# Attention reads and an expert layer on one core: the order of quadrant sums, state products and read transposes

## The chip, the cores and the metric

The kernel runs on one core of a Trainium2 chip. The metric is the device time of one execution in microseconds (us), taken as the median of several runs; less is better. The engines are TensorE (PE), VectorE (DVE), ScalarE (ACT), GpSimd (POOL) and SyncE (SP), which only issues DMAs here. Each engine works through its own list of instructions in order, and semaphores order the engines among each other.

## The reference

A cross-attention between a sequence and a small state, in both directions, is followed by an expert layer with an exact gelu. There are 8 batches, 8 heads, 512 positions, 32 state rows and 64 values a head.

```python
scores = scale * x @ state.T            # per batch and head
xread = softmax(scores) @ state         # 512 rows
sread = softmax(scores.T) @ x           # 32 rows
y = concat([xread, sread])              # (8 * 544, 512), heads side by side
g = gelu(y @ w_in)                      # w_in  512 x 2048
out = g @ w_out                         # w_out 2048 x 512
```

## The kernel before

The instruction order is written out by hand: the scheduler leaves the lists as the Python code emits them. Batches 0 and 1 are worked through by a start-up section. A loop then goes over batches b = 2 to 7; one pass is called a slot here, and each slot has eight steps p = 0 to 7 (units 1 to 8).

**State products (P).** Instead of forming the read and then multiplying it by w_in, the kernel multiplies the state by w_in. `p_mm(b, f, tiles)` makes chunk f (512 of the 2048 columns) of batch b: 8 matmuls of 64x32 weights into two PSUM tiles, one for each t (half of the heads). `p_copy` casts tile t = 0 on ACT and t = 1 on DVE to the bf16 tensor P. In most slots all four chunks of the next batch are made in step 5 by `p_all`, together with the state's reads (sr). For batch 2 chunks 0 and 1 are made ahead of the loop, and chunks 2 and 3 in slot 2 by `pmat`.

**Hidden layer.** `M(k, k + 1)` computes two of the 16 blocks (128 hidden values by 512 positions): two matmuls hp from P and the transposed attention weights AT, then a gelu on ACT into g. Block m needs chunk m // 4 of P. Step p makes blocks 2p and 2p + 1.

**Second layer.** g @ w_out runs by seven products of quadrants instead of eight. `X(b, name)` is one product: 16 matmuls xp into one PSUM bank. The names are 3, 4, 5, 2, 1, 6 and 7. Products 5, 2, 1, 6 and 7 need a sum of two quadrants of g, made on DVE by `g_sum` (128 x 2048 bf16, a pool of three buffers), called g5, g2, g1, g6 and g7 below. Product 6 needs only blocks 0 to 7. In slot b steps 0 to 3 and 5 run products 4, 5, 1, 2 and 7 of batch b - 1, step 5 ends with product 3 of batch b and step 7 with product 6 of batch b.

What follows a product: X3 is copied to s3 on ACT; X4 is added on DVE (s34); X5 is copied on ACT (oh), and POOL makes u; X1 is added on DVE (q); X2 is copied on ACT (oh), POOL makes v, and DVE adds (L618); X7 is added on DVE (L654). SP writes the results out.

**State reads.** `reads_mm` computes sr on PE, ACT copies it (sraw), `reads_norm` scales it on DVE to srm; `srt` transposes srm on PE (srT) and DVE copies it into XSR. In the last slot (read-out, batch 7) the rows of all reads go through the expert layer (sp, srx, srw, rp). Slot 6 handles the reads of batches 6 and 7.

**Order of the rest of a slot.** Scores of batch b + 1 come in step 1, the norms in steps 2 and 3 on DVE, the DMA transposes on SP in steps 3 and 5. POOL waits at `hold_for` for a gelu, issues the loads of x and rearranges x (L225 and L235) between its u and v.

**PSUM.** The pool `ps_f` has four buffers, taken in turn by hp, scores, sr, srT and those P tiles that name no place. The pool `ps_o` has four named places o0 to o3, one bank each; X3 and X5 use o0, X4 and X2 use o1, X1 and X7 use o2, X6 uses o3. `p_all` puts chunks 0 to 3 at (o0, ps_f), (ps_f, ps_f), (o1, o3) and (o2, ps_f).

The parts of the slot that matter here, in step order:

```python
M(k, k + 1)
if b == 2 and p in (0, 3):
    pmat(2, 2 + p // 3)
...
    if p == 3:
        g_sum(b, "6")
    X(b - 1, "45127"[p])
```

Of the kernel before, what the change touches and what calls it, by code (L numbers as in the profile page):

```python
# [10 lines left out]
BF16 = mybir.dt.bfloat16  # L11
# [6 lines left out]
def kernel(  # L18
# [8 lines left out]
    nc = tc.nc  # L27

    B, H, S, D = x.shape
    _, _, NS, _ = state.shape  # L30
# [3 lines left out]
    HC = H // 2  # L34
# [13 lines left out]
    ps_f = ctx.enter_context(tc.tile_pool(name="ps_f", bufs=4, space=PSUM))  # L48
# [6 lines left out]
    def otile(shape, name, at=None):  # L55
        if at is None:
            at = turn[0] % 4
            turn[0] += 1
        return ps_o.tile(shape, FP32, name=name, tag=f"o{at}")

    def ftile(shape, name):
        return ps_f.tile(shape, FP32, name=name, tag="f")
# [5 lines left out]
    ident = persist.tile([128, 128], BF16, name="ident")  # L68
    sbd = persist.tile([128, B, HC, 2 * NS], BF16, name="sbd")
    XSR = persist.tile([128, HC, NS, B], BF16, name="XSR")  # L70
# [133 lines left out]
    atts = {}  # L204
# [25 lines left out]
    def rearr_ones(b):  # L230
        A = atts[b]
        eng = nc.vector if b < 2 else nc.gpsimd
        src = xbs[b].rearrange("p (t c) (j d) -> p t c j d", t=2, d=D)
        for t in range(2):
            eng.tensor_copy(  # L235
                out=A.xo[:, :, :, 2 + 64 * t:66 + 64 * t].rearrange("p j c d -> p c j d"),
                in_=src[:, t],
            )
# [174 lines left out]
    def srt(b):  # L413
        A = atts[b]
        ps = ps_f.tile([128, HC, NS], BF16, name="srT", tag="f")
        nc.tensor.transpose(  # L416
            ps.rearrange("p c n -> p (c n)"), A.srm.rearrange("q t d -> q (t d)"), ident
        )
        nc.vector.tensor_copy(out=XSR[:, :, :, b], in_=ps)  # L419

    Ps = {}

    def p_mm(b, f, tiles):
        if b not in Ps:
            Ps[b] = att.tile([128, 2, d_ff], BF16, name="P", tag="P")
        ps = [tiles([128, 512], "p_ps") for t in range(2)]
        for c in range(HC):
            for t in range(2):
                nc.tensor.matmul(  # L429
                    ps[t][32 * c:32 * c + 32, :],  # L430
                    lhsT=sbd[64 * t:64 * t + 64, b, c, 32 * t:32 * t + 32],
                    rhs=w_in_bf[64 * t:64 * t + 64, c, f * 512:(f + 1) * 512],
                    start=True,
                    stop=True,
                )
        return ps

    def p_copy(b, f, ps):
        dst = Ps[b][:, :, f * 512:(f + 1) * 512]
        nc.scalar.copy(out=dst[:, 0, :], in_=ps[0])  # L440
        nc.vector.tensor_copy(out=dst[:, 1, :], in_=ps[1])  # L441

    def pmat(b, f):
        p_copy(b, f, p_mm(b, f, ftile))
# [134 lines left out]
    def g_q(b, h, k):  # L579
        return gs[b][:, MH * k:MH * k + MH, 256 * h:256 * h + 256]  # L580

    def g_sum(b, name):
        (h0, k0), (h1, k1), op = G_SUMS[name]
        t = apool.tile([128, MH, 256], BF16, name="gsum", tag="gsum")
        nc.vector.tensor_tensor(out=t, in0=g_q(b, h0, k0), in1=g_q(b, h1, k1), op=op)  # L585
        xs[b, "g" + name] = t
# [34 lines left out]
    def X(b, name):  # L621
        bank = {"3": 0, "4": 1, "5": 0, "2": 1, "1": 2, "6": 3, "7": 2}[name]
        first = name in "3416"
        if first:
            xs[b, bank] = otile([128, 2, NH], "xp", bank)
        ps = xs[b, bank]
        lhs = {"3": (0, 0), "4": (1, 1)}.get(name)
        lhs = xs[b, "g" + name] if lhs is None else g_q(b, *lhs)
        rhs = {"5": w_q[1][1], "2": w_q[0][0]}.get(name)
        rhs = w_sum[name] if rhs is None else rhs  # L630
        x_mm(ps, lhs, rhs, first)
        if name == "3":
            xs[b, "s3"] = c_tile("s3")
            if b > 1:
                nc.scalar.copy(out=xs[b, "s3"], in_=ps)
            for h in range(2):
                xs[b, "o", h] = hpool.tile([128, 2, d_model], FP32, name="oh", tag=f"oh{h}")
        elif name == "4":
            xs[b, "s34"] = c_tile("s34")
            nc.vector.tensor_tensor(out=xs[b, "s34"], in0=ps, in1=xs[b, "s3"], op=ALU.add)  # L640
        elif name == "5":
            o = xs[b, "o", 0][:, :, NH:]
            nc.scalar.copy(out=o, in_=ps)  # L643
            xs[b, "u"] = c_tile("u")
            x_out(b, 0, right)
            nc.gpsimd.tensor_tensor(out=xs[b, "u"], in0=xs[b, "s34"], in1=o, op=ALU.subtract)  # L646
        elif name == "2":
            nc.scalar.copy(out=xs[b, "o", 1][:, :, :NH], in_=ps)  # L648
            c22(b)
        elif name == "1":  # L650
            xs[b, "q"] = c_tile("q")
            nc.vector.tensor_tensor(out=xs[b, "q"], in0=ps, in1=xs[b, "s34"], op=ALU.add)  # L652
        elif name == "7":
            nc.vector.tensor_tensor(  # L654
                out=xs[b, "o", 0][:, :, :NH], in0=ps, in1=xs[b, "u"], op=ALU.add
            )
            x_out(b, 0, left)
# [268 lines left out]
                op=ALU.mult,  # L926
            )

    def p_all(b, bs):
        raw = reads_mm(bs)  # L930
        done = []
        for f, at in enumerate(((0, None), (None, None), (1, 3), (2, None))):
            it = iter(at)

            def tiles(shape, name):
                i = next(it)
                return ftile(shape, name) if i is None else otile(shape, name, i)

            done.append((b, f, p_mm(b, f, tiles)))
        for x in done:  # L940
            p_copy(*x)
        reads_norm(bs, raw)

    def p_copy_v(b, f, ps):
# [7 lines left out]
    def M(*ms):  # L952
        for m in ms:
            mm1(m // MC, m % MC)
# [198 lines left out]
    for b in range(2, B):  # L1153
        nb = b + 1
        for p in range(8):
            k = 16 * b + 2 * p
            if p == 1 and nb < B:
                scores(nb, 0)
                scores(nb, 1)
            if p in (2, 3) and nb < B:  # L1160
                norm(nb, p - 2)
            if p == 3 and nb + 1 < B:
                xtr_dma(nb + 1)
            if p == 5 and nb < B:
                atr_dma(nb)
            if p == 7 and nb < B:
                srt(b)
                if nb == B - 1:
                    srt(nb)
            if nb == B and p < 5:  # L1170
                read_out_slot(p)
                if p == 4:
                    r_homes()
                    r_sum("5")
                    r_sum("2")
                continue
            M(k, k + 1)
            if b == 2 and p in (0, 3):
                pmat(2, 2 + p // 3)
            if b == 2 and p == 1:  # L1180
                w_sums(4)
            if p < 4 or (p == 4 and nb == B):
                if p == 0:
                    g_sum(b - 1, "5")
                    if b > 2:
                        sr_w("5216"[b - 3])
                if p == 3:
                    g_sum(b, "6")
                X(b - 1, "45127"[p])
                if p < 3:  # L1190
                    g_sum(b - 1, "127"[p])
            if p == 0 and b + 3 < B:
                hold_for(b, 0)
                load_x(4 if b == 2 else b + 3)
            if p == 6 and b == 2:
                hold_for(b, 12)
                load_x(5)
            if p == 0 and nb + 1 < B:
                begin(nb + 1)
                rearr(nb + 1)  # L1200
            if nb == B:
                if p == 5:
                    g_sum(b, "6")
                    R("3")
                    r_sum("1")
                    R("4")
                    r_sum("6")
                    r_sum("7")
                if p == 6:
                    R("5")  # L1210
                    X(b, "3")
                    R("2")
                    R("1")
                if p == 7:
                    R("6")
                    X(b, "6")
                continue
            if p == 5:
                X(b - 1, "7")
                reads = (b, nb) if nb == B - 1 else (b,)  # L1220
                p_all(nb, reads)
                if b == 2:
                    rearr_ones(3)
                elif nb + 1 < B:
                    rearr_ones(nb + 1)
                X(b, "3")
            if p == 7:
                if b == 2:
                    rearr_ones(4)
                X(b, "6")  # L1230
    b = B - 1
    for name in "521":
# [39 lines left out]
```

## Time and profile before

| | us |
|---|---|
| median of 3 runs | 205.29 (205.24 to 205.36) |
| the profiled execution | 205.13 |
| its span in the trace | 203.2 |
| PE busy | 196.0 (96%) |
| DVE busy | 162.9 (80%) |
| ACT busy | 136.6 (67%) |
| POOL busy | 68.4 (34%) |
| DVE quadrant sums (gsum), 35 | 50.2, mean 1.449 |
| DVE casts of P, 29 | 18.3, mean 0.681 |
| ACT casts of P, 29 | 15.3, mean 0.597 |
| DVE copies into XSR, 8 | 5.7, mean 0.758 |

Times in the trace count from the start of the span. The slots begin at about 50 us (slot 2), 73, 95, 116, 137 and 159 us (slots 3 to 7). Rows of a timeline give start, length, engine, line, operation, tiles and shapes and the count of merged instructions; a bracket at the end names idle time before the row and what released it. Matmuls of one kind are pipelined, so their rows overlap by a tail, and start-to-start distances are the pace.

### The profile page before, as it was taken

To read this page: it belongs to the slowest core of one execution; us is meant where nothing else is said; L and a number is where in the kernel's file an instruction comes from. 1 tells how busy PE (TensorE), PEld (TensorE's weight loads), DVE (VectorE), ACT (ScalarE), POOL (GpSimd) and SP (SyncE) were. 2 spreads that over 40 slices of the span, in tenths; PEclk is the share of its full clock that TensorE was granted. 3 is DMA by queue.
4 is the path that set the end of the run, shared out by engine and by line. 5 is a ranking of instruction groups with operands and counts; after the bars stand their busy time and mean duration, and the time that the engine had idled before them with its cause. 6 is when DMAs were issued, how large, how long until landed. Compare 5 with 4: busy or idle time off the path is not lost.

```text
span 203.2 us, 4901 instructions
## 1 busy us (share of the span) xinstructions
PE 196.0 (96%) x2030; PEld 133.9 (66%) x2035; DVE 162.9 (80%) x255; ACT 136.6 (67%) x245; POOL 68.4 (34%) x75
## 2 busy tenths in 40 slices
PE   7899999999999999999999999999999999999993
PEld 2434544466766687666776677677776887878893
DVE  2954876789999889996899777967799888895882
ACT  3785678798985779656967597687857576864120
POOL 8972503324259297430527302420220002200000
PEclk9999999999999999999999999999999999999999
DMA  6999999986655879633772508270107001040134
GB/s 192 199 172 203 206 198 197 185 163 126 89 104 106 206 87 143 135 126 84 94 167 77 133 0 127 39 205 0 52 3 206 3 0 55 0 158 0 52 107 155
DMA packets 40566, 23.16 MB, mean 114 GB/s; under 512 B 21856, under 2 KB 39136, under 8 KB 40544
## 3 DMA queue, kind: packets, MB, share of 16 engines
q0 software_dynamic: 13984, 8.10, 29.3%
q1 hardware_dynamic: 25872, 14.36, 27.7%
q10 hardware_dynamic: 688, 0.39, 0.6%
q8 instruction: 16, 0.26, 0.5%
q14 instruction: 6, 0.05, 0.1%
HBM read 17.30 MB, written 8.91 MB: 129 GB/s over the span
## 4 chain that ended last, share of the span: by engine, by line
PE 68%; DVE 15%; DMA 5%; POOL 4%; issue 4%; ACT 2%; DVEq 0%; POOLq 0%; ACTq 0%
PE xp L591 30%; PE hp L494 20%; DVE gsum L585 6%; DMA xb<-in_x_dram 5%; PE op L536 3%; PE sp L798 3%; PE rp L864 3%; POOL w_in_bf L105 2%; DVE P L441 2%; DVE a L356 2%; PE op L520 2%; PE xp L703 2%; PE p_ps L429 2%; DVE cs L353 1%; PE pt L333 1%
## 5 line engine op out<-in xcount | busy, mean ns | idle before, releaser
L501 ACT ACTIVATE g<-hp 128x512 bf16<-128x512 f32 x124 | 66.3, 606 | 21.5 <-PE hp L494 17.0
L494 PE MATMUL hp<-AT,P 128*128 128x512 bf16 x248 | 62.0, 379 | 0.6 <-DVE P L441 0.4
L591 PEld LDWEIGHTS <-gsum 128*128 128x128 bf16 x528 | 51.4, 98 | 11.4 <-DVE q L652 0.2
L585 DVE TENSOR_TENSOR gsum<-g 128x2048 bf16<-128x2048 bf16 x35 | 50.2, 1449 | 4.1 <-ACT g L501 4.0
L494 PEld LDWEIGHTS <-P 128*128 128x128 bf16 x248 | 23.2, 98 | 21.1 <-issue 2.2
L591 PE MATMUL xp<-ws,gsum 128*128 128x256 bf16 x304 | 36.3, 273 | 0.0
L591 PE MATMUL xp<-ws,g 128*128 128x256 bf16 x224 | 26.8, 273 | 0.2
L591 PE MATMUL xp<-w_out_bf,gsum 128*128 128x256 bf16 x224 | 26.6, 273 | 0.0
L591 PEld LDWEIGHTS <-g 128*128 128x128 bf16 x224 | 21.5, 98 | 5.0 <-issue 1.6
L646 POOL TENSOR_TENSOR u<-s,oh 128x512 f32<-128x512 f32 x6 | 8.8, 1467 | 40.6 <-ACT oh L643 40.6
L225 POOL COPY x<-xb 128x1024 bf16<-128x1024 bf16 x12 | 14.3, 1225 | 16.6 <-DMA xb<-in_x_dram 16.6
L441 DVE CAST P<-p_ps 128x512 bf16<-128x512 f32 x29 | 18.3, 681 | 1.2 <-PE p_ps L429 1.0
L440 ACT CAST P<-p_ps 128x512 bf16<-128x512 f32 x29 | 15.3, 597 | 4.8 <-PE p_ps L429 4.7
L235 POOL COPY xo<-xb 128x1024 bf16<-128x1024 bf16 x12 | 13.2, 1129 | 5.0 <-PE sr L905 5.0
L610 POOL TENSOR_TENSOR v<-q,oh 128x512 f32<-128x512 f32 x6 | 8.2, 1371 | 19.6 <-ACT oh L648 17.2
L356 DVE TENSOR_TENSOR a<-e,ics 128x512 bf16<-128x512 bf16 x14 | 11.7, 833 | 0.5
L536 PE MATMUL op<-w_out_bf,g 128*128 128x512 bf16 x44 | 11.1, 380 | 0.5 <-issue 0.3
L353 DVE TENSOR_REDUCE cs<-e 128x16 f32<-128x512 bf16 x14 | 9.5, 677 | 0.7 <-ACT e L340 0.7
L429 PE MATMUL p_ps<-w_in_bf,sbd 64*32 64x512 bf16 x248 | 9.6, 381 | 0.3 <-DVE oh L654 0.3
L501 ACT ACT_TABLE_LOAD x7 | 9.0, 1283 | 0.1
L419 DVE COPY XSR<-srT 128x128 bf16<-128x128 bf16 x8 | 5.7, 758 | 3.8 <-PE srT L416 3.8
L536 PEld LDWEIGHTS <-g 128*128 128x128 bf16 x48 | 4.1, 97 | 5.9 <-issue 1.1
(137 smaller groups left out, 233.2 us busy)
## 6 DMA issues: line engine op xcount, KB each, us to landing
out_dram<-oh SPq DMA_DIRECT2D x15, 256.0 KB, 2.7
xb<-in_x_dram POOLq DMA_DIRECT2D x7, 512.0 KB, 7.5
out_dram<-oh SPq DMA_DIRECT2D x6, 512.0 KB, 2.8
w_in_bf<-in_moe_w_in_dram POOLq DMA_DIRECT2D x6, 256.0 KB, 11.8
out_dram<-osb SPq DMA_DIRECT2D x5, 256.0 KB, 3.2
w_out_bf<-in_moe_w_out_dram POOLq DMA_DIRECT2D x4, 256.0 KB, 8.0
w_out_bf<-in_moe_w_out_dram POOLq DMA_DIRECT2D x2, 512.0 KB, 13.3
x0f<-in_x_dram SPq DMA_DIRECT2D x3, 256.0 KB, 3.8
```

Source lines behind the costliest of these rows:

```text
L225: nc.gpsimd.tensor_copy(out=A.x4[:, :, :, 64 * t:64 * t + 64].rearrange("p j c d -> p c j d"), in_=src[:, t],)
L235: eng.tensor_copy(out=A.xo[:, :, :, 2 + 64 * t:66 + 64 * t].rearrange("p j c d -> p c j d"), in_=src[:, t],)
L353: nc.vector.reduce_sum(out=cs, in_=e4, axis=AX.X)
L356: nc.vector.tensor_tensor(out=A.a[:, :, hs].rearrange("p g (c n) -> p g c n", n=NS), in0=e4, in1=ics[:, :, :].to_broadcast((128, G, 2, NS) ...
L429: nc.tensor.matmul(ps[t][32 * c:32 * c + 32, :], lhsT=sbd[64 * t:64 * t + 64, b, c, 32 * t:32 * t + 32], rhs=w_in_bf[64 * t:64 * t + 64, c ...
L440: nc.scalar.copy(out=dst[:, 0, :], in_=ps[0])
L441: nc.vector.tensor_copy(out=dst[:, 1, :], in_=ps[1])
L494: nc.tensor.matmul(hp, lhsT=Ps[b][:, t, m * 128:(m + 1) * 128], rhs=atts[b].AT[:, :, t, :], start=(t == 0), stop=(t == 1),)
L501: nc.scalar.activation(out=gs[b][:, m, :], in_=hp, func=AF.Gelu)
L536: nc.tensor.matmul(ops[b, j], lhsT=gs[b][:, m, j * 128:(j + 1) * 128], rhs=w_out_bf[:, m, :], start=(m == 0), stop=(m == MC - 1),)
L585: nc.vector.tensor_tensor(out=t, in0=g_q(b, h0, k0), in1=g_q(b, h1, k1), op=op)
L591: nc.tensor.matmul(ps[:, j - js[0], :], lhsT=lhs[:, m, 128 * j:128 * j + 128], rhs=rhs[:, m, :], start=(first and j == js[0] and m == 0), ...
```

## The change

Four things are different.

1. In `p_all`, tile t = 1 of chunk 0 is cast on ACT instead of DVE. ACT makes five of the eight casts, DVE three.
2. `g_sum(b, "6")` is no longer emitted in step 3 of slots 2 to 6, ahead of X2, but in step 5, behind `p_all` and its norm.
3. `srts` replaces `srt`: the transposes of srm come in step 7 behind that step's two blocks and ahead of X6, no longer ahead of the blocks. In slot 6 both transposes go into one PSUM tile, and one DVE copy takes them.
4. In slot 2, chunks 2 and 3 of batch 2's P are no longer made in steps 0 and 3. Step 2 makes blocks 4 to 7 at once, then X1 and g7, then both chunks in one run of 16 matmuls with their four casts. Step 3 then has no blocks left to make.

The number of matmuls is the same. Five P casts move from DVE to ACT, and one XSR copy fewer remains on DVE.

```diff
+    def srts(bs):
+        ps = ps_f.tile([128, len(bs), HC, NS], BF16, name="srT", tag="f")
+        for i, b in enumerate(bs):
+            nc.tensor.transpose(
+                ps[:, i].rearrange("p c n -> p (c n)"),
+                atts[b].srm.rearrange("q t d -> q (t d)"),
+                ident,
+            )
+        nc.vector.tensor_copy(
+            out=XSR[:, :, :, bs[0]:bs[-1] + 1], in_=ps.rearrange("p b c n -> p c n b")
+        )
...
-    def p_all(b, bs):
+    def p_all(nb, bs):
...
-            done.append((b, f, p_mm(b, f, tiles)))
-        for x in done:
-            p_copy(*x)
+            done.append((nb, f, p_mm(nb, f, tiles)))
+        for b, f, ps in done:
+            for t in range(2):
+                copy = nc.scalar.copy if t == 0 or f == 0 else nc.vector.tensor_copy
+                copy(out=Ps[b][:, t, f * 512:(f + 1) * 512], in_=ps[t])
         reads_norm(bs, raw)
...
-            if p == 7 and nb < B:
-                srt(b)
-                if nb == B - 1:
-                    srt(nb)
...
-            M(k, k + 1)
-            if b == 2 and p in (0, 3):
-                pmat(2, 2 + p // 3)
+            if b != 2 or p != 3:
+                M(k, k + 1)
+            if b == 2 and p == 2:
+                M(k + 2, k + 3)
+                X(1, "1")
+                g_sum(1, "7")
+                for x in [(2, f, p_mm(2, f, ftile)) for f in (2, 3)]:
+                    p_copy(*x)
...
-                if p == 3:
-                    g_sum(b, "6")
-                X(b - 1, "45127"[p])
-                if p < 3:
-                    g_sum(b - 1, "127"[p])
+                if b > 2 or p != 2:
+                    X(b - 1, "45127"[p])
+                    if p < 3:
+                        g_sum(b - 1, "127"[p])
...
                 p_all(nb, reads)
+                g_sum(b, "6")
...
             if p == 7:
                 if b == 2:
                     rearr_ones(4)
+                srts(reads)
                 X(b, "6")
```

## The prediction

> **What bounds the kernel now.** I read the shares first, then the chain of waits, then the timelines of TensorE (PE), VectorE (DVE), ScalarE (ACT) and GpSimd (POOL) around the edited lines.
>
> ```profile
> PE 196.0 (96%) x2030; PEld 133.9 (66%) x2035; DVE 162.9 (80%) x255; ACT 136.6 (67%) x245; POOL 68.4 (34%) x75
> PEclk9999999999999999999999999999999999999999
> ```
>
> PE is the bound, at a full granted clock. No matmul count changes, so the change can only win or lose time in which PE stands. The rows below show where PE stands; all lie before 158 us. The chain of waits from 156.99 us to 195.70 us is PE alone, so what is won before is carried to the end.
>
> Slot 2 (the pass over batch 2), PE timeline; columns are start, length, line, tiles, count, and idle before with its releaser:
>
> ```profile
> 51.16 0.41 PE L429 MATMUL p_ps<-w_in_bf,sbd 64*32 64x512 bf16 x8
> 59.91 0.41 PE L429 MATMUL p_ps<-w_in_bf,sbd 64*32 64x512 bf16 x8
> 62.00 1.46 PE L494 MATMUL hp<-AT,P 128*128 128x512 bf16 x6
> 63.87 0.59 PE L494 MATMUL hp<-AT,P 128*128 128x512 bf16 x2 [0.40 <-DVE P L441]
> 64.30 1.91 PE L591 MATMUL xp<-ws,gsum 128*128 128x256 bf16 x16
> ```
>
> The lengths hold a pipeline tail, so I reckon from start to start: hp costs 0.216 a matmul (x8 is 1.73 in the chain), X 1.75 for x16. Six hp from 62.00 should end at 63.30; the next comes at 63.87, so PE stands 0.57 for DVE's cast of chunk 3.
>
> Slot 3, PE and then DVE:
>
> ```profile
> 88.99 0.41 PE L429 MATMUL p_ps<-w_in_bf,sbd 64*32 64x512 bf16 x8 [0.19 <-DVE oh L654]
> 89.33 1.92 PE L591 MATMUL xp<-ws,g 128*128 128x256 bf16 x16
> ```
>
> ```profile
> 86.52 1.21 DVE L585 TENSOR_TENSOR gsum<-g 128x2048 bf16<-128x2048 bf16 x1
> 87.66 0.68 DVE L618 TENSOR_TENSOR oh<-xp,v 128x512 f32<-128x512 f32 x1
> 88.26 0.68 DVE L654 TENSOR_TENSOR oh<-xp,u 128x512 f32<-128x512 f32 x1
> ```
>
> The first of these is g6 in its old place. It pushes L654, which frees PSUM tag o2, and the last of the four P chunks in `p_all` waits for o2.
>
> Slot 4 (DVE, POOL) and slot 6 (PE):
>
> ```profile
> 112.92 0.74 DVE L922 TENSOR_TENSOR srm<-sraw,inv 128x128 bf16<-128x128 f32 x1
> ```
>
> ```profile
> 111.49 2.03 POOL L225 COPY x<-xb 128x1024 bf16<-128x1024 bf16 x2
> ```
>
> ```profile
> 156.46 0.36 PE L416 MATMUL srT<-ident,srm 128*128 128x128 bf16 x2
> 156.99 1.10 PE L494 MATMUL hp<-AT,P 128*128 128x512 bf16 x4 [0.17 <-ACT g L501]
> ```
>
> In slot 6 two srT tiles make the next hp wait for a buffer that a gelu frees.
>
> **Slot 2, the two P runs joined behind unit 2.** Removed: two runs of x8. The first costs 51.07 (end of the hp from 50.21) to 51.50 (next X), 0.43; the second the same; 0.86 together. Added: one x16 run. The one at 45.88 runs from the hp end at 45.79 to the hp at 46.44: 0.65. Saved 0.21.
>
> Walk PE from 51.07 without gaps: X4 1.75, scores 0.47, two blocks 0.86, X5 1.75, blocks 4 to 7 1.73, X1 1.75, P run 0.65, X2 1.75. That is 61.78; block 8's first half ends at 62.00 and its second needs chunk 2's cast on DVE. DVE's order there is norm, q, g7, then the two casts. X1 ends near 59.4 as against 58.95, and q stood at 59.48 behind norm's multiply anyway, so I leave g7 at 60.09 plus its 1.45, which ends at 61.5. The cast of 0.68 ends near 62.15, and PE goes on at 62.2: a stall of 0.2 replaces the 0.57. X7 starts at 62.2 + 7 x 0.216 = 63.7 or 63.75, against 64.30: **0.55 won**. Lower end: if g7 slides by the 0.45 of X1's shift, 0.1. Upper end: no stall at all, 0.21 + 0.57 = 0.78. I take 0.55, since norm's row bounds q on both sides of the change.
>
> Covers: blocks 6 and 7 take the PSUM buffers of blocks 2 and 3, whose gelus end 56.3 and 56.9 by ACT's rows (the exp table load moves from 52.48 to 52.0 when the cast at 51.87 leaves); PE wants them at 56.8 and 57.2. The P run takes those of blocks 4 to 7, free by 59.3; wanted at 59.5 and 59.7. If one gelu (0.5) is late, 0.1 to 0.3 is lost. Norm's second half and the POOL-fed add L618 queue behind the casts on DVE. L618 then ends near 65.6, L654 near 66.3, the chunk that needs o2 comes at 66.57. SP's transpose of batch 3's weights (median 3.9 to land) is issued about 1.4 later, behind that norm, and would land near 69 for a first use after 72: hidden. POOL's holds, loads and copies keep their order.
>
> **`p_all` in slots 2 to 6, one cast from DVE to ACT.** ACT gains five casts at 0.49 start to start (four take 2.05), DVE loses five at 0.60 (four take 2.47). ACT's cover is its wait ahead of the s3 copy: 1.01 in slot 3, 0.82 in slot 4, 0.58 each in slots 2 and 6, so nothing; uncovered it would be at most 0.49 in a slot, but only through a gelu that PE waits for. The first ACT cast, which frees X3's bank, keeps its place.
>
> **g6 behind `p_all`.** In its old place it goes away from before L618 and L654. Slot 3: L654 then follows X7's end (87.35) and is done near 88.2; the fourth chunk comes at 88.39 (its pace after the third), and X3 is bound by ACT's first cast, 88.27 + 0.59 + 0.06 = 88.92, against 89.33: **0.41 won**. Slot 4 has the same stall: X3 at 110.60 against 110.82, 0.22, but see the next lines. Slots 2, 5 and 6 show no such stall.
>
> In its new place X6 waits for it. From L654's end or the second chunk's latency (0.5 after its matmuls start, as in slot 6): three casts, inv, srm, then g6 1.21. Against X6's natural start:
> - slot 2: g6 done 70.1, X6 at 70.7 (0.5 in hand);
> - slot 3: 92.0 against 92.5;
> - slot 5: 135.4 against 135.9;
> - slot 6, two norms: 157.3 against 157.5;
> - slot 4: casts end 112.1, but srm meets POOL's pair of copies 111.49 to 113.52. Before, srm ended at 113.66 instead of some 0.3 after its start. If it ends there again, g6 ends at 114.8 and X6 starts at 114.86 against 114.81 before: 0.05 lost, and the 0.22 with it. If srm slips in between the copies, the second copy moves by 0.3 and g6 ends at 115.0: 0.24 lost. If neither meets POOL, X6 starts at 114.2: 0.6 won. I take **0.1 lost**, by the srm row.
>
> The Trainium skill (SBUF — State Buffer, Who interferes with whom) speaks against this place: a VectorE instruction with two SBUF inputs and a GpSimd instruction that reads SBUF exclude each other for a whole instruction, and who issues first goes first. The rows of slot 4 agree (srm 0.74 there, 0.29 in slot 3), and so does a gsum of 3.17 beside the POOL copies at 72.29. By the rule alone, whose copies come as a queue of whole instructions, slot 4 loses 0.24 instead of 0.1.
>
> **srT behind the slot's last two blocks.** Slot 6: the hp at 156.99 no longer waits for gelu 12, because srT is allocated after it. Lost there before: 156.99 less 156.72 and the tails, by pace 0.34 + 0.08 = **0.42 won**; 0.49 if the 0.07 between the two transposes also goes, 0 if srT only moves the wait. Its new tile needs gelu 12, done 156.9, wanted 157.3. Slot 4's wait of srT for srm is counted above. The other srT move at no cost (0.06 each). On DVE the XSR copies move behind g6; slot 6 has one of 256 strided elements for two of 0.73 (1.30 together). Between 0.73 and 1.46, I take 1.3: done 159.1, the two srx 159.6, wanted by the first read-out matmul near 160.1. That margin of 0.5 is thin but uncovered only by a late g6.
>
> **Sum.** 0.55 + 0.41 - 0.10 + 0.42 = 1.28. The profiled execution took 205.13 (span 203.2); 205.13 - 1.28 = 203.85. The median 205.29 lies 0.16 above, giving 204.0.
>
> **Rivals.**
> - Slot 4 free (no meeting with POOL): 0.7 more, 203.3. Against it, srm's row.
> - Only half comes: slot 2 wins 0.1 and slot 6 nothing; 0.1 + 0.41 - 0.1 = 0.4, so 204.9. For it: g7 and norm on DVE are already at the limit in slot 2.
> - Nothing arrives: DVE or ACT in the read-out slot 7 eats it, 205.3. PE's gapless chain speaks for slack, but shows only that there is some.
> - Slower: g6 becomes X6's gate in all five slots. Beside a POOL instruction a gsum takes 2.29 (slot 4's old g6), 1.1 more. Margins 0.5, 0.5, 0.5 and 0.2 would turn into losses of 0.6, 0.6, 0.6 and 0.9, and slot 4 into 1.2 in place of 0.1: 3.8 against wins of 1.28 + 0.1, net 2.5, so 207.8. It decides from about 0.75 a slot. Against it: POOL idles at those times in slots 2, 3, 5 and 6 (3.56 before the hold at 70.87, nothing from 89.86 to 96.14, none near 134 or 156).
>
> **How the numbers follow.** Forecast 0.52, slot 4 free 0.16, half 0.15, nothing 0.08, slower 0.09. The range 203.2 to 204.95 takes the first three with their bounds. A difference of 0.2% (0.41) is about what a measurement of this kernel can tell from none: faster 0.80, same 0.10, slower 0.10.
>
> **What would show it.** Right: no wait of hp for P over 0.3 in slot 2, the four P chunks of slots 3 and 4 in one x32 row, hp x8 ahead of srT in slot 6 without a gelu wait, X6 in slot 4 the only one to wait for gsum. Wrong: L591 waiting for DVE gsum L585 at X6 in slots 2, 3, 5 or 6; ACT's s3 copy starting after X3's end by over 0.6; a gap in slot 7, where there was none.

## The result and the profile after

The changed kernel takes 203.93 us (203.59 to 204.46) where the kernel before takes 205.26 (204.95 to 206.0): a ratio of 0.9933, with a 95% interval of 0.9911 to 0.9954. A further comparison of the same two kernels, on one chip, gave 0.9941 (0.9917 to 0.9965). The profiled execution took 203.66, with a span of 201.6.

The shares, from the page of the changed kernel:

```profile
PE 195.0 (97%) x2030; PEld 134.3 (67%) x2035; DVE 156.0 (77%) x249; ACT 138.8 (69%) x250; POOL 68.0 (34%) x75
```

DVE has lost 6.9 us of work, ACT gained 2.2, and the kernel got 1.3 shorter. The shares do not say where; PE's standing time does. Line numbers are those of the changed kernel here: p_ps is L441, hp L506, X is L603, gsum L597, the casts of `p_all` L955.

Slot 2 on PE (start, length, line, tiles, count, idle before):

```profile
59.28 0.62 PE L441 MATMUL p_ps<-w_in_bf,sbd 64*32 64x512 bf16 x16
59.84 1.92 PE L603 MATMUL xp<-w_out_bf,gsum 128*128 128x256 bf16 x16
61.60 0.38 PE L506 MATMUL hp<-AT,P 128*128 128x512 bf16 x1
62.23 1.68 PE L506 MATMUL hp<-AT,P 128*128 128x512 bf16 x7 [0.25 <-DVE P L453]
63.75 1.91 PE L603 MATMUL xp<-ws,gsum 128*128 128x256 bf16 x16
```

The two P runs are one. A wait for a cast is still there: the first half of block 8 starts at 61.60, the second at 62.23 instead of 61.82, so 0.41 is lost where 0.57 was. What the cast waited for is on DVE:

```profile
59.39 0.69 DVE L664 TENSOR_TENSOR q<-xp,s 128x512 f32<-128x512 f32 x1 [0.78 <-PE xp L603]
60.00 1.57 DVE L597 TENSOR_TENSOR gsum<-g 128x2048 bf16<-128x2048 bf16 x1
61.49 1.27 DVE L453 CAST P<-p_ps 128x512 bf16<-128x512 f32 x2
```

DVE stands 0.78 for the end of X1; then q, g7 and only then the casts. In the kernel before, the norm's multiply (`a`) ended later and q followed it without a wait:

```profile
58.54 1.02 DVE L356 TENSOR_TENSOR a<-e,ics 128x512 bf16<-128x512 bf16 x1
59.48 0.68 DVE L652 TENSOR_TENSOR q<-xp,s 128x512 f32<-128x512 f32 x1
60.09 1.45 DVE L585 TENSOR_TENSOR gsum<-g 128x2048 bf16<-128x2048 bf16 x1
```

Slot 3, PE and ACT. The four chunks run as one row of 32. The first of ACT's five casts, which frees X3's bank, ends at 88.28 (87.69 + 0.59), and X3 follows 0.05 later:

```profile
87.22 1.06 PE L441 MATMUL p_ps<-w_in_bf,sbd 64*32 64x512 bf16 x32
88.33 1.91 PE L603 MATMUL xp<-ws,g 128*128 128x256 bf16 x16
```

```profile
87.69 2.54 ACT L955 CAST P<-p_ps 128x512 bf16<-128x512 f32 x5
```

Slot 4, DVE, POOL and PE. This is the one place where X6 waits for g6:

```profile
111.14 0.47 DVE L934 TENSOR_TENSOR srm<-sraw,inv 128x128 bf16<-128x128 f32 x1
111.54 2.05 DVE L597 TENSOR_TENSOR gsum<-g 128x2048 bf16<-128x2048 bf16 x1
```

```profile
110.44 2.08 POOL L225 COPY x<-xb 128x1024 bf16<-128x1024 bf16 x2
```

```profile
113.65 1.92 PE L603 MATMUL xp<-ws,gsum 128*128 128x256 bf16 x16 [0.42 <-DVE gsum L597]
```

The pair of copies ends at 112.52. g6 ends at 113.59, 1.07 after that, so it did next to nothing while the second copy ran (a gsum without a copy beside it takes 1.22). X6 of slot 4 in the kernel before, to which the account of the prediction comes back:

```profile
114.64 1.91 PE L591 MATMUL xp<-ws,gsum 128*128 128x256 bf16 x16
```

Slot 6, PE and DVE:

```profile
154.57 1.89 PE L506 MATMUL hp<-AT,P 128*128 128x512 bf16 x8
156.30 0.28 PE L424 MATMUL srT<-ident,srm 128*128 128x128 bf16 x2
156.41 1.91 PE L603 MATMUL xp<-ws,gsum 128*128 128x256 bf16 x16
```

```profile
156.61 0.43 DVE L429 COPY XSR<-srT 128x256 bf16<-128x256 bf16 x1 [0.35 <-PE srT L424]
```

The four blocks of steps 6 and 7 run without a gap, srT waits for nothing, and one copy of 0.43 stands for two that took 1.30 in the kernel before:

```profile
156.71 1.30 DVE L419 COPY XSR<-srT 128x128 bf16<-128x128 bf16 x2 [0.18 <-PE srT L416]
```

A yardstick without the noise of the kernel's ends is the stretch from the state transposes ahead of slot 2 (the last row of L160) to the start of X6 in slot 6: 109.76 before, 108.41 after, 1.35 less. The table gives it for all kernels, with the two distances in a slot that move: sr (its first matmul) to X3, and X3 to X6. All are start to start in the traces of one execution each, in us.

| kernel | stretch | to sr of slot 2 | slot 2 | slot 3 | slot 4 | slot 5 | slot 6 |
|---|---|---|---|---|---|---|---|
| before | 109.76 | 17.95 | 1.52 + 3.56 | 1.89 + 3.58 | 1.70 + 3.83 | 1.47 + 3.56 | 1.74 + 4.08 |
| changed | 108.41 | 17.59 | 1.52 + 3.53 | 1.47 + 3.53 | 1.47 + 4.11 | 1.47 + 3.53 | 1.74 + 3.58 |
| changed, again | 108.41 | 17.58 | 1.52 + 3.53 | 1.47 + 3.53 | 1.47 + 4.11 | 1.47 + 3.53 | 1.74 + 3.58 |
| slot 2 alone | 110.31 | 17.59 | 2.45 + 3.58 | 1.88 + 3.58 | 1.70 + 3.83 | 1.47 + 3.56 | 1.73 + 4.08 |
| g6 and casts alone | 109.82 | 17.92 | 1.52 + 3.56 | 1.47 + 3.56 | 1.47 + 4.12 | 1.47 + 3.56 | 1.73 + 4.55 |
| srT alone | 108.78 | 17.89 | 1.52 + 3.53 | 1.88 + 3.54 | 1.69 + 3.54 | 1.47 + 3.53 | 1.73 + 3.58 |
| four casts each | 108.85 | 17.59 | 1.52 + 3.53 | 1.47 + 3.53 | 1.47 + 4.26 | 1.47 + 3.53 | 1.74 + 3.87 |
| g6 back | 109.43 | 17.58 | 2.46 + 3.54 | 1.88 + 3.54 | 1.69 + 3.54 | 1.47 + 3.53 | 1.73 + 3.58 |
| batch 7 later | 107.81 | 17.58 | 1.52 + 3.53 | 1.47 + 3.53 | 1.47 + 3.53 | 1.47 + 3.53 | 1.74 + 3.58 |
| casts before g7 | 107.98 | 17.16 | 1.52 + 3.53 | 1.47 + 3.53 | 1.47 + 4.11 | 1.47 + 3.53 | 1.73 + 3.58 |
| both | 107.39 | 17.16 | 1.52 + 3.52 | 1.47 + 3.53 | 1.47 + 3.53 | 1.47 + 3.53 | 1.74 + 3.58 |
| both, again | 107.39 | 17.16 | 1.52 + 3.53 | 1.47 + 3.53 | 1.47 + 3.53 | 1.47 + 3.53 | 1.74 + 3.58 |
| both, srT ahead | 108.50 | 17.16 | 1.52 + 3.56 | 1.47 + 3.56 | 1.47 + 3.56 | 1.47 + 3.56 | 1.74 + 4.55 |

### The profile page after: what moved, and what is told of

The parts are those of the page before. It is cut to its first block, busy times and chain, and to the rows that moved or that the text cites. A ratio compares the mean times of both kernels' runs of the same rounds, so it can differ in the third digit from the quotient of the medians.

```text
span 201.6 us, 4900 instructions
## 1 busy us (share of the span) xinstructions
PE 195.0 (97%) x2030; PEld 134.3 (67%) x2035; DVE 156.0 (77%) x249; ACT 138.8 (69%) x250; POOL 68.0 (34%) x75
## 4 chain that ended last, share of the span: by engine, by line
PE 88%; DVE 6%; ACT 2%; DMA 2%; issue 1%; ACTq 0%
PE xp L603 39%; PE hp L506 26%; PE op L548 5%; PE sp L810 3%; PE rp L876 3%; PE p_ps L441 2%; PE op L532 2%; PE xp L715 2%; DVE gsum L597 2%; DMA st_f<-in_state_dram 2%; PE pt L333 2%; PE sr L917 1%; ACT P L955 1%; DVE P L955 1%; PE hp L1060 1%
## 5 line engine op out<-in xcount | busy, mean ns | idle before, releaser
L506 PE MATMUL hp<-AT,P 128*128 128x512 bf16 x248 | 61.2, 379 | 0.3 <-DVE P L453 0.2
L603 PEld LDWEIGHTS <-gsum 128*128 128x128 bf16 x528 | 51.2, 98 | 11.5 <-DVE gsum L597 0.8
L597 DVE TENSOR_TENSOR gsum<-g 128x2048 bf16<-128x2048 bf16 x35 | 47.5, 1371 | 0.5
L506 PEld LDWEIGHTS <-P 128*128 128x128 bf16 x248 | 23.3, 98 | 21.6 <-DVE P L453 1.0
L603 PE MATMUL xp<-ws,gsum 128*128 128x256 bf16 x304 | 36.3, 273 | 0.4 <-DVE gsum L597 0.4
L603 PE MATMUL xp<-ws,g 128*128 128x256 bf16 x224 | 26.7, 272 | 0.3
L603 PE MATMUL xp<-w_out_bf,gsum 128*128 128x256 bf16 x224 | 26.6, 273 | 0.0
L603 PEld LDWEIGHTS <-g 128*128 128x128 bf16 x224 | 21.8, 98 | 5.3 <-issue 1.6
L235 POOL COPY xo<-xb 128x1024 bf16<-128x1024 bf16 x12 | 12.6, 1080 | 5.0 <-PE sr L917 5.0
L955 ACT CAST P<-p_ps 128x512 bf16<-128x512 f32 x25 | 12.7, 606 | 0.1
L955 DVE CAST P<-p_ps 128x512 bf16<-128x512 f32 x15 | 9.4, 685 | 1.7 <-PE p_ps L441 1.7
L441 PE MATMUL p_ps<-w_in_bf,sbd 64*32 64x512 bf16 x248 | 8.8, 380 | 0.0
L452 ACT CAST P<-p_ps 128x512 bf16<-128x512 f32 x9 | 4.9, 589 | 5.4 <-PE p_ps L441 5.4
L963 POOL COPY hold<-g 128x1 bf16<-128x1 bf16 x5 | 2.9, 575 | 16.9 <-ACT g L513 16.8
```

Source lines behind the costliest of these rows:

```text
L235: eng.tensor_copy(out=A.xo[:, :, :, 2 + 64 * t:66 + 64 * t].rearrange("p j c d -> p c j d"), in_=src[:, t],)
L441: nc.tensor.matmul(ps[t][32 * c:32 * c + 32, :], lhsT=sbd[64 * t:64 * t + 64, b, c, 32 * t:32 * t + 32], rhs=w_in_bf[64 * t:64 * t + 64, c ...
L506: nc.tensor.matmul(hp, lhsT=Ps[b][:, t, m * 128:(m + 1) * 128], rhs=atts[b].AT[:, :, t, :], start=(t == 0), stop=(t == 1),)
L603: nc.tensor.matmul(ps[:, j - js[0], :], lhsT=lhs[:, m, 128 * j:128 * j + 128], rhs=rhs[:, m, :], start=(first and j == js[0] and m == 0), ...
L955: copy(out=Ps[b][:, t, f * 512:(f + 1) * 512], in_=ps[t])
```

## The experiments

The theory was the prediction's: each part moves a wait of PE of its own. The rival was that the gain comes of the load on DVE, whose busy time fell by 6.9. Line numbers in rows are those of the kernel that the row is from; in kernels made from the one before, p_ps is L429, hp L494, X L591 and gsum L585.

**Slot 2 alone**, on the kernel before:

```diff
-            M(k, k + 1)
-            if b == 2 and p in (0, 3):
-                pmat(2, 2 + p // 3)
+            if b != 2 or p != 3:
+                M(k, k + 1)
+            if b == 2 and p == 2:
+                M(k + 2, k + 3)
+                X(1, "1")
+                g_sum(1, "7")
+                for x in [(2, f, p_mm(2, f, ftile)) for f in (2, 3)]:
+                    p_copy(*x)
...
-                X(b - 1, "45127"[p])
-                if p < 3:
-                    g_sum(b - 1, "127"[p])
+                if b > 2 or p != 2:
+                    X(b - 1, "45127"[p])
+                    if p < 3:
+                        g_sum(b - 1, "127"[p])
```

> The kernel before with the slot 2 part alone (chunks 2 and 3 of batch 2's P in one run behind unit 3, blocks 4 to 7 ahead). Theory (PE's gaps decide, each part has its own): the joined run wins 0.21 and the wait for the cast shrinks from 0.57 to about 0.4, so 0.37; g6 is still ahead of L618 in slot 2, where it may push L654 and cost up to 0.3 of it: 204.9 to 205.2. Slots 3, 4 and 6 keep their stalls. Rival (the gain comes of taking casts from DVE): no cast is moved, so no gain, 205.3.

206.08 us, ratio 1.0038 (1.0017 to 1.0059): slower. The 0.36 ahead of slot 2's sr came as in the changed kernel, but `p_all` then lost 0.93. PE, DVE and POOL of this run:

```profile
67.29 0.41 PE L429 MATMUL p_ps<-w_in_bf,sbd 64*32 64x512 bf16 x7 [0.33 <-DVE oh L618]
67.88 0.41 PE L429 MATMUL p_ps<-w_in_bf,sbd 64*32 64x512 bf16 x8 [0.19 <-DVE oh L654]
```

```profile
64.58 2.05 DVE L585 TENSOR_TENSOR gsum<-g 128x2048 bf16<-128x2048 bf16 x1
```

```profile
64.06 3.48 POOL L235 COPY xo<-xb 128x1024 bf16<-128x1024 bf16 x2
```

In the kernel before, g6 of slot 2 started earlier and took less:

```profile
63.74 1.68 DVE L585 TENSOR_TENSOR gsum<-g 128x2048 bf16<-128x2048 bf16 x1
```

Two casts instead of one stand between X1 and g6 on DVE now. g6, in its old place, starts 0.84 later and takes 2.05 beside POOL's copies, and both PSUM places that L618 and L654 free come late: two chunks wait instead of none. The cost was expected at 0.3 at most; it was three times that. The DVE-load rival said no effect, which is wrong too.

**g6 and casts alone**, on the kernel before: `g_sum(b, "6")` moved behind `p_all`, five casts on ACT (not shown here; as in the change).

```diff
...
-                if p == 3:
-                    g_sum(b, "6")
...
                 p_all(nb, reads)
+                g_sum(b, "6")
```

> The kernel before with g6 behind p_all and five casts on ACT, nothing else. Theory: slot 3's wait of the fourth chunk goes (0.41), slot 4 comes out level, slot 2 and slot 6 keep their waits (0.57 and 0.42): 204.85. Rival (DVE load): this part holds nearly all of the DVE time that was saved, so most of the 1.33: 204.1.

205.49 us, ratio 1.0003 (0.9984 to 1.0023): no difference. This part holds most of the relief of DVE (162.9 to 156.9 us busy; the whole change reaches 156.0) and wins nothing, so the load rival falls. Slot 3 won its 0.42 and slot 4 came out near level, as expected. What was not expected is slot 6, which lost 0.47. PE and DVE there:

```profile
156.35 0.59 PE L494 MATMUL hp<-AT,P 128*128 128x512 bf16 x2 [0.25 <-ACT g L501]
157.33 0.59 PE L494 MATMUL hp<-AT,P 128*128 128x512 bf16 x2 [0.39 <-DVE XSR L419]
```

```profile
155.43 1.22 DVE L585 TENSOR_TENSOR gsum<-g 128x2048 bf16<-128x2048 bf16 x1
156.56 1.29 DVE L419 COPY XSR<-srT 128x128 bf16<-128x128 bf16 x2
```

The slot's last block takes the buffer of the first srT, and that is free only when its XSR copy has run. The first of the two copies ends at 157.28 here and PE goes on 0.05 later; the copies stand behind g6 on DVE.

**srT alone**, on the kernel before: `srts(reads)` ahead of X6 in step 7 for `srt` ahead of the blocks.

```diff
...
-            if p == 7 and nb < B:
-                srt(b)
-                if nb == B - 1:
-                    srt(nb)
...
+                srts(reads)
                 X(b, "6")
```

> The kernel before with srT behind the slot's last two blocks, nothing else. Theory: slot 6 wins 0.42 to 0.49 (no hp behind gelu 12), slot 4 wins its wait of srT for srm, 0.27, since X6 has its sum early in this kernel: 204.5. Rival (DVE load): one XSR copy of 0.7 less, no gain, 205.3.

204.14 us, ratio 0.9929 (0.9911 to 0.9948). Slot 6 won 0.50 and slot 4 0.29, as expected; amounts of 0.02 to 0.06 in each of the other slots make the rest of 0.98. This part alone is about as fast as the whole change: the intervals overlap, and by the stretch it lacks 0.37. It does this with DVE still 161.3 us busy, which speaks against the load rival once more.

**Four casts each**, on the changed kernel: `p_copy(b, f, ps)` for the copies in `p_all`.

```diff
-            for t in range(2):
-                copy = nc.scalar.copy if t == 0 or f == 0 else nc.vector.tensor_copy
-                copy(out=Ps[b][:, t, f * 512:(f + 1) * 512], in_=ps[t])
+            p_copy(b, f, ps)
```

> The changed kernel with four casts of p_all on each engine again. Theory: DVE starts its first cast in time in which it waited (0.28 in slots 2 and 3, 0.5 in slot 6), so g6 comes 0.3 later, not 0.6; margins hold in slots 2, 3 and 5, slot 6 loses 0.2, slot 4 0.1 to 0.2: 204.2. Rival (DVE load): the casts are the cause, 204.9 to 205.3.

204.5 us, ratio 0.995 (0.9926 to 0.9974). Slots 2, 3 and 5 lose nothing, slot 4 loses 0.15 and slot 6 0.29: 0.44 in the stretch where 0.3 to 0.4 was expected. In slot 4 srm starts in the second half of a pair of POOL copies (110.65 to 112.68) and ends only 0.14 after the pair; in the changed kernel it got in between the two:

```profile
111.74 1.08 DVE L934 TENSOR_TENSOR srm<-sraw,inv 128x128 bf16<-128x128 f32 x1
```

**Batch 7 later**, on the changed kernel: POOL's rearrangement for batch 7 waits for the first gelu of batch 5.

```diff
                 begin(nb + 1)
+                if b == 5:
+                    hold_for(b, 0)
                 rearr(nb + 1)
```

> The changed kernel with one hold more on POOL: the rearrangement of batch 7's x waits for the first gelu of batch 5, so its two copies no longer lie in slot 4 beside srm and g6. Theory (g6 is blocked by the copies): g6 of slot 4 takes 1.2 instead of 2.05 and X6's wait of 0.59 goes, 203.35; the copies then lie in slot 5 beside g5 and srw, where PE has no wait today, or 0.2 if they delay g1. Rival (X6 in slot 4 waits because DVE is late anyway): 203.9.

203.34 us, ratio to the kernel before on that chip 0.9931 (0.9904 to 0.9958). The changed kernel had 0.9933 in its own comparison, so the medians alone do not show a gain; the trace does. DVE and POOL:

```profile
111.46 1.22 DVE L597 TENSOR_TENSOR gsum<-g 128x2048 bf16<-128x2048 bf16 x1
```

```profile
116.64 2.02 POOL L225 COPY x<-xb 128x1024 bf16<-128x1024 bf16 x2
```

With the copies gone from beside it, g6 takes 1.22 for 2.05, X6 waits for nothing, and slot 4 is 0.58 shorter (0.60 by the stretch). PE shows no new wait in slot 5.

**Casts before g7**, on the changed kernel, in slot 2:

```diff
-                g_sum(1, "7")
                 for x in [(2, f, p_mm(2, f, ftile)) for f in (2, 3)]:
                     p_copy(*x)
+                g_sum(1, "7")
```

> The changed kernel with g7 behind the four casts in slot 2. Theory: the casts start when q ends, chunk 2 is there before block 8, the stall of 0.41 goes and X7 has its g7 in time: 203.5. Rival (blocks 8 to 11 wait for ACT's gelus or PSUM anyway): 203.9.

203.38 us, ratio 0.9928 (0.9904 to 0.9952); here too the gain is read from the trace. The casts follow q at once, and blocks 8 to 11 run as one row of eight:

```profile
60.03 1.28 DVE L453 CAST P<-p_ps 128x512 bf16<-128x512 f32 x2
```

```profile
61.62 1.89 PE L506 MATMUL hp<-AT,P 128*128 128x512 bf16 x8
```

The stall of 0.41 is gone (17.16 against 17.59 to slot 2's sr), and X7 finds its g7.

**Both**, the two edits together:

> Both of the last two together. Theory: the two waits are apart in time and add up, 1.0 less than the changed kernel: 202.95. Rival: one is only moved to a later wait, 203.4 to 203.6.

203.06 us beside 203.34 and 203.38 for the single edits; ratio to the kernel before 0.9907 (0.9881 to 0.9934). Next to the changed kernel on one chip, once more:

> The changed kernel once more, beside the next two on the same chip, since a tenth of a per cent is at stake: 0.993 to 0.995 of the kernel before.

> The changed kernel with g7 behind the casts and the later rearrangement of batch 7, beside the changed kernel on the same chip. Theory (the two waits were 0.41 and 0.59 and nothing took their place): 1.0 under the changed kernel. Rival (the end of the kernel, the last writes, eats part): 0.4 to 0.6 under it.

204.09 for the changed kernel and 203.42 for both edits. By the stretch the two waits add up in full (107.39 against 108.41, 1.02), twice over. By these medians the gain is 0.67, between the 1.0 of the theory and the 0.4 to 0.6 of its rival. The trace shows one thing that blurs medians of this size: from X6 of slot 6 to the last instruction, with the matmuls alike to 0.02, the two executions of the changed kernel took 45.11 and 45.85, those of both edits 45.72 and 45.19. The last write landed 1.7 and 2.5 after its issue in the first pair, 2.3 and 1.8 in the second. So the wait for the last write differs between executions, not the kernel.

**g6 back** in step 3, all else as changed:

```diff
+                if p == 3:
+                    g_sum(b, "6")
                 if b > 2 or p != 2:
                     X(b - 1, "45127"[p])
...
                 p_all(nb, reads)
-                g_sum(b, "6")
```

> The changed kernel with g6 back in step 3, all else as changed. Theory: slot 3's fourth chunk waits again (0.41 lost) and slot 4's (0.22 lost), slot 4's X6 no longer waits (0.59 won), slot 2's L654 comes late (0 to 0.4 lost): 204.0 to 204.4. Rival (the place of g6 is the whole gain): 205.2.

205.52 us, ratio 1.0023 (1.0002 to 1.0044), outside what was expected. Slots 3 and 4 did as expected; slot 2 lost 0.94, as in the kernel with slot 2 alone. By its stretch this kernel should still be 0.33 under the kernel before, but its median is 0.52 over that kernel's 205.0 on the same chip. Its profiled execution (204.88), in which the last part took the short 45.11, lies 0.12 under that. The spread of the last writes (0.74 between two executions above) could cover most of these 0.85; only one execution was traced, so this is open.

**Both edits, srT ahead** of the blocks again:

> The kernel with both waits taken away, with the read transposes back ahead of the blocks (srT in step 7 before blocks 14 and 15, as in the kernel before). Theory (with g6 behind the casts the XSR copies come late, and the last block of slot 6 waits for the buffer that they free): slot 6 loses 0.9 to 1.0, as in the kernel that had g6 and the casts alone, slots 2 to 5 lose nothing: 0.9 above the kernel with both. Rival (srT's place is worth the 0.42 of the prediction whatever stands around it): 0.45 above.

204.65 us on the chip where both edits took 203.42. The stretch is 1.11 longer. Slot 6 lost 0.97 from X3 to X6, with the same two waits as in the kernel with g6 and the casts alone; slots 2 to 5 lost 0.03 to 0.04 each. The wait for the XSR copy is:

```profile
156.17 0.59 PE L506 MATMUL hp<-AT,P 128*128 128x512 bf16 x2 [0.39 <-DVE XSR L419]
```

## Why the prediction came out

The sum was 1.28; the stretch shortened by 1.35 and the median by 1.33. The forecast of 204.0 stands against 203.93. The mechanism, standing times of PE that each part moves, is what the runs show. That the total came so close is in part luck: the four terms measure 1.23, with slot 2 too high and slots 4 and 6 too low in the sum, and the other 0.12 are small gains in the other distances, which the prediction put at nothing. By its steps:

- **Slot 2: 0.55 forecast, 0.36 measured.** The joined run saved the 0.21. The stall that stays was put at 0.2 and is 0.41. The step that was mis-sized is DVE's way to the cast: the text bounded q by norm's multiply and left g7 at its old time, with 1.45. But a P run and its cast on DVE (51.67 before) have left the start of the slot, and norm's multiply is 0.33 shorter, so norm ends early, at 58.61, and the row of q shows DVE waiting for X1, 0.2 past X1's end; g7 then took 1.57. With the two traces laid over each other at the stretch's start (48.18 before, 48.00 after), q is 0.09 later than before and g7 0.12 longer, which is the 0.21 that the stall has over its forecast. From X1's end to the cast's result is 0.2 + 0.61 + 1.49 + 0.68 + 0.06 = 3.04, and PE has 0.65 + 1.75 + 0.22 = 2.62 of other work: 0.42. It does not need the other three parts: the kernel with slot 2 alone shows the same 0.41. The sign given for being right, no wait of hp for P over 0.3, holds by the bracket in the row (0.25) and not by the pace (0.41).
- **Slot 3: 0.41 forecast, 0.42 measured,** by the mechanism named: moving g6 with the casts alone brings it, and putting g6 back loses it.
- **Slot 4: 0.1 lost forecast, 0.05 measured** (0.23 won up to X3, 0.28 lost to X6). srm did slip in at the end of the first copy (0.47), but the second copy hardly moved, so g6 ended earlier than in that case of the prediction. The case that was chosen, srm behind both copies, did not come. It was also set against a wrong start: 114.81 is X6's start in the chain of waits, while PE's row has 114.64, by which the chosen case would have lost 0.22. So the number here is near by luck. That POOL's copies are the cause was argued then; it is shown by the run that moved them away, in which slot 4 wins 0.53 over the kernel before (5.53 to 5.00 from sr to X6), close to the 0.6 of the case without POOL.
- **Slot 6: 0.42 forecast, 0.50 measured.** Of the 0.08 between them 0.07 is the gap between the two transposes (0.13 from start to start before, 0.06 after), which the prediction named and left out (its 0.49). One step was half seen: the wait for gelu 12 was named, but the 0.08 inside its 0.42, booked as a tail, is the last block's wait for the first XSR copy. That copy ends at 157.44 in the kernel before, and the last block starts at 157.50 instead of 157.42. The wait is that small only because the copy had no g6 ahead of it. The two runs with g6 behind the casts and srT ahead of the blocks show it at about 0.55.
- **Margins at X6** in slots 2, 3, 5 and 6 held, so g6 did not become the gate, and the slower rival did not come (its losses add up to 3.9 and not 3.8; the net of 2.5 stands). With four casts on DVE, slot 6's margin is gone at once.
- **The XSR copy** of slot 6, taken at 1.3, is 0.43.

What the sum could not show is that the parts need each other. Alone they are worth +0.55, +0.06 and -0.98 on the stretch, together -0.37; the change brings -1.35. Slot 2's order pays only with g6 out of the way (0.93), and g6's new place costs nothing in slot 6 only with srT behind the blocks (0.97 in the last run). The prediction worked out each step in the presence of the others, and so did not see this.

The Trainium skill (SBUF — State Buffer, Who interferes with whom) has a VectorE instruction with two SBUF inputs and a reading GpSimd instruction exclude each other for a whole instruction. The runs agree: g6 of slot 4 took 2.05 beside the copy and 1.22 without it, and the difference of 0.83 is near the 0.98 of the copy that it overlapped.

## What to carry to other kernels

When one engine is busy nearly all the time, list the times in which it stands, by start-to-start pace, and work out for each what comes second last: that is what it waits for once the first wait is gone. Cost a moved step together with its neighbours in the queue of the engine that it moves on, and not part by part. Two placements paid in this kernel: work that frees a PSUM buffer went ahead of long sums in the vector engine's queue, and the taker of a buffer that is freed late went to the end of the run. A sum that must be in time should not share its stretch with copies on GpSimd: one more hold that moved a pair of copies won 0.60 of the stretch, where the whole change won 1.35.

## What the runs showed of the hardware that was not expected

- One XSR copy of 128x256 elements, written in pairs of neighbours, took 0.43 where two of 128x128, written in single elements with a stride, took 0.73 each (1.30 together): the same number of elements in a third of the time. Other causes than the pairs were not tried.
- The wait for the last write differs by 0.7 between two executions of one kernel (45.11 and 45.85 from the same matmul), which is more than half of what this change brought.
- A DVE sum can wait for both of two POOL copies: g5 of slot 2 in the changed kernel took 3.17 from 71.70, beside a pair of copies from 71.75 to 73.78, while srm in slot 4 got in after the first copy of a pair (0.47). By the rows g5 starts 0.05 ahead of the pair and yet waits for both, which does not fit the prediction's "who issues first goes first"; starts this close settle nothing. What decides was not tried.
